# A Conformer block on one core: scores with keys on partitions, folded key weights and DMA transposes in place of the row-maximum softmax

## The chip, the cores and the metric

The kernel runs on one core of one Trainium2 chip. The metric is the device time of one execution in microseconds (us), the median of several runs. A core has five engines with a queue of instructions each: TensorE (PE in the profile, with its weight loads as PEld), VectorE (DVE), ScalarE (ACT), GpSimd (POOL) and SyncE (SP). Each queue is worked off in order. The engines meet through semaphores only.

## What is computed

```
x: 2 x 4000 x 512 bf16;  F = 2048;  LN(v) = (v - mean) / sqrt(var + 1e-5), no gain
x1 = x + 0.5 * silu(LN(x) @ w_ff1_a) @ w_ff1_b
h  = LN(x1);  q, k, v = h @ w_q, h @ w_k, h @ w_v
x2 = x1 + softmax(q k^T / sqrt(512)) v @ w_o            # one head, 4000 keys per batch
a, b = split(LN(x2) @ w_pw1);  g = a * sigmoid(b)
dc = depthwise conv of g over time, 3 taps (dw)
dc = (dc - mean) / sqrt(var + 1e-5) per channel, over all 8000 tokens
x3 = x2 + silu(dc) @ w_pw2
x4 = x3 + 0.5 * silu(LN(x3) @ w_ff2_a) @ w_ff2_b
out = LN(x4)
```

## The kernel before

The 8000 tokens are 64 tiles of 125 and 16 chunks of 500; a batch is 8 chunks. The residual stream (XT) stays in SBUF in bf16 with tokens on partitions. A small class (`Sync`) counts semaphores: each operation waits for what it reads and overwrites, in the order in which the program is written out. The block is four phases with barriers between them, and each phase allocates its own SBUF and PSUM.

**Layer norm** (L348 to L408). For each of a chunk's four tiles DVE takes statistics (`bn_stats` L353, `bn_aggr` L356); DVE adds epsilon (L359), and POOL makes the reciprocal root and the shift in three small operations (L362, L365, L368). ACT normalises each tile (L379). The features must then be on partitions: PE transposes each tile in four 125x128 pieces (L394, 16 to a chunk) into PSUM, and DVE copies them out (L407).

**Feed-forward, twice** (L460). For each chunk, 16 groups f: four matmuls (L533) make 128 hidden features by 500 tokens, ACT takes the sigmoid (L537), DVE multiplies (L540), and three groups later four matmuls (L555) add the group's share to four token tiles in PSUM. The residual enters through four more matmuls with twice the identity as weights (L551), and ACT copies the halved sum back to XT (L419). The layer norm of a chunk is prepared while the chunks before it are worked on.

**Attention** (L618). K^T, q^T and v' = h (Wv Wo) are projected for all chunks of a batch (L671, L696); q^T goes to DRAM and back (L687, L729). Then there are 128 tasks to a batch: a query tile of 125 against 1000 keys. PE makes scores with queries on partitions (L742), DVE takes their row maximum (L757) and updates the running one, ACT takes exp with the maximum as bias and sums (L787), PE transposes the eight blocks of probabilities (L818), DVE copies them (L827), PE multiplies by v' (L839), and DVE rescales and adds to the running output (L855). Scores are issued two tasks ahead.

**Convolution** (L1013). For each chunk: four pairs of gated projections (L1085, sigmoid L1089, product L1094), the layer norm of the next chunk mixed in between the pairs (one ACT normalisation behind each sigmoid), and the depthwise taps of two chunks before as diagonal matmuls (L1136), which ACT copies (L1140) and DVE takes statistics of (L1143). After all chunks the channel statistics are finished and a second loop does the normalisation, silu (L1205, L1209, L1213) and the last projection (L1229).

The order in one attention step and in one convolution step is written out by hand:

```
MX(n+1) EX(n+1) TR(n) CP(n) SC(n+2) PV(n) RL(n) OU(n-1)          # attention, task n
pw1_pair(tc, jj, lprev); stats at jj 0; transposes at jj 1 and 3   # convolution, chunk tc
```

Of the kernel before, what the change touches and what calls it, by code (L numbers as in the profile page):

```python
# [5 lines left out]
F32 = mybir.dt.float32  # L6
BF16 = mybir.dt.bfloat16
ALU = mybir.AluOpType
AF = mybir.ActivationFunctionType
AX = mybir.AxisListType  # L10

TILE = 125
CHUNK = 500
TPC = CHUNK // TILE
KEYBANK = 500
KBPC = 2
FF_LAG = 3
# [11 lines left out]
class Buf:  # L29
    __slots__ = ("name", "w", "r", "excl")  # L30
# [6 lines left out]

    def __repr__(self):
        return "Buf(%s)" % self.name


class Sync:
# [3 lines left out]
    def __init__(self, nc, n_dma_sems=32):  # L46
# [23 lines left out]
        self.stats = {"waits": 0, "instrs": 0, "multi": 0}  # L70

    def _required(self, reads, writes):
# [14 lines left out]
        for b in writes:  # L87
            add(b.w)
            for ev in b.r.values():
                add(ev)  # L90
        return req
# [9 lines left out]
    def _emit_waits(self, e, req):  # L101
        clk = self.clock[e]
        n = 0
        for key in sorted(req, key=str):
# [8 lines left out]
            n += 1  # L113
        self.stats["waits"] += n
        if n > 1:
            self.stats["multi"] += 1
# [8 lines left out]
    def op(self, e, fn, reads=(), writes=(), inc=True):  # L125
# [3 lines left out]
        self.stats["instrs"] += 1  # L129
# [21 lines left out]
    def dma(self, e, dkey, fn, reads=(), writes=()):  # L151
# [8 lines left out]
        self.stats["instrs"] += 1  # L160
# [13 lines left out]
    def barrier(self, engines=None):  # L174
        if engines is None:
            engines = self.ENGS
        targets = dict((k, v) for k, v in self.count.items() if v > 0)
        for e in engines:
            for key, val in targets.items():
                if key == e:  # L180
                    continue
                self.wait_event(e, Ev(key, val, {}))


def conformer_kernel(nc, x, w_ff1_a, w_ff1_b, w_q, w_k, w_v, w_o, w_pw1, dw, w_pw2,
                     w_ff2_a, w_ff2_b, out, phases=None):
    if phases is None:
        phases = dict(ff1=True, att=True, conv=True, ff2=True)
    B, T, D = x.shape
    F = w_ff1_a.shape[1]  # L190
    KW = dw.shape[0]
    N = B * T
    assert D == 512 and T % CHUNK == 0 and N % TILE == 0 and KW % 2 == 1 and KW < CHUNK
    DC = D // 128
    FC = F // 128
    NT = N // TILE
    NCK = N // CHUNK
    TCB = T // CHUNK
    TB = T // TILE
    SCALE = float(D) ** -0.5  # L200
    EPS = 1e-5
    PAD = KW // 2

    x_flat = x.rearrange("b t d -> (b t) d")
    out_flat = out.rearrange("b t d -> (b t) d")

    S = Sync(nc)
    uid = [0]

    def sbuf(stack, shape, dtype):  # L210
        uid[0] += 1
        return stack.enter_context(nc.sbuf_tensor("sb%d" % uid[0], shape, dtype))

    psum_banks = {}

    def psum(stack, shape, dtype):
        uid[0] += 1
        h = stack.enter_context(nc.psum_tensor("ps%d" % uid[0], shape, dtype))
        mloc = nc.lookup_mloc(h)
        psum_banks[h.name] = (mloc.bank, nc.num_psum_banks(shape, dtype))  # L220
        return h

    PSUM_PREFIXES = ("hps", "yps", "prj", "vpp", "sps", "ptp", "ops", "pwp", "dcps", "y2", "plnT", "dwps")

    def nbuf(prefix):
        uid[0] += 1
        return Buf("%s%d" % (prefix, uid[0]), excl=(prefix in PSUM_PREFIXES))

    with ExitStack() as gstack:
        XT = sbuf(gstack, [TILE, NT, D], BF16)  # L230
        bx = [Buf("x%d" % g) for g in range(NT)]
        ident = sbuf(gstack, [128, 128], BF16)
        bid = Buf("ident")
        ident2 = sbuf(gstack, [128, 128], BF16)
        bid2 = Buf("ident2")
        neghalf = sbuf(gstack, [128, 4], F32)
        bneghalf = Buf("neghalf")
        epsc = sbuf(gstack, [128, 4], F32)
# [9 lines left out]
        def _(_eng):  # L248
# [17 lines left out]
            def load_x(n_chunks):  # L266
                for _ in range(n_chunks):
                    tc = xload_state["next"]
                    if tc >= NCK:
                        return  # L270
# [1075 lines left out]
```

## Time and profile before

| | |
|---|---|
| device time, median of 3 runs | 2513.72 us (2510.93 to 2516.74) |
| span of the profiled execution | 2512.2 us |
| mean granted TensorE clock | 0.985 |
| PE busy | 95% of the span, 13220 matmuls |
| DVE busy | 71%, 4261 instructions |
| ACT busy | 47%, 2536 instructions |
| POOL busy | 5%, 255 instructions |
| DMA moved | 47.05 MB, all issued by SP |

The profile is of one execution, which lasted 2512.2 us from its first to its last instruction; the device time of the runs is about 1.5 us more. "busy" is the time in which an engine ran at least one instruction, and matmuls overlap each other. The chain of waits follows the work that ended last back in time, and says of each stretch which engine and line it was spent on. The timeline gives start and duration in us, engine, line, operation, operands and, in brackets, how long the engine had been idle before and for whom it waited. A window row gives for each engine the busy time and, in brackets, the instructions.

### The profile page before, as it was taken

The page shows a single profiled execution, that of the slowest core. Times are in us where ns is not written, and L with a number is a line of the kernel's source. Part 1 is how long each engine was busy: PE and PEld are TensorE (multiplying, and loading weights), DVE is VectorE, ACT ScalarE, POOL GpSimd, SP SyncE. Part 2 cuts the span into 40 slices and gives each one's busy share as a digit, 9 for nine tenths or more (in the row PEclk, how much of TensorE's full clock was granted, in tenths as well). Part 3 has the DMA queues.
Part 4 walks back from the last instruction along what each step waited for, and adds up shares of the span by engine and source line. Part 5 has one row for each costly group of instructions (what it writes and reads, how often), then busy time and mean ns, then how long its engine had stood idle before and what let it go on. Part 6 is the DMA issues. An engine that isn't in the chain of part 4 may idle for free.

```text
span 2512.2 us, 34795 instructions
## 1 busy us (share of the span) xinstructions
PE 2383.2 (95%) x13220; PEld 1429.3 (57%) x13220; DVE 1779.5 (71%) x4261; ACT 1185.9 (47%) x2536; POOL 115.2 (5%) x255
## 2 busy tenths in 40 slices
PE   5999999989999999989999999996998979999997
PEld 3555555544666666655566666664443545555554
DVE  4555555464888888887588888887887966666664
ACT  3544444444333333336433333333665845555554
POOL 0000000000000000001000000000110001000100
PEclk9999999999999999999999999998999989999999
DMA  4100000011000000001100000000000020000000
GB/s 156 43 1 1 1 1 1 4 63 51 9 9 9 9 9 9 1 1 42 42 9 9 9 9 9 9 1 26 1 1 1 1 68 17 17 17 19 23 17 25
DMA packets 44874, 47.05 MB, mean 19 GB/s; under 512 B 1057, under 2 KB 44196, under 8 KB 44708
## 3 DMA queue, kind: packets, MB, share of 16 engines
q1 hardware_dynamic: 44708, 44.83, 5.6%
q8 instruction: 105, 1.72, 0.3%
q14 instruction: 61, 0.50, 0.1%
HBM read 28.45 MB, written 16.38 MB: 18 GB/s over the span
## 4 chain that ended last, share of the span: by engine, by line
PE 90%; ACT 4%; DVE 3%; DMA 1%; SPq 1%; issue 1%; POOL 0%; ACTq 0%; POOLq 0%; DVEq 0%
PE ps L839 18%; PE ps L555 17%; PE ps L742 17%; PE ps L533 17%; PE ps L818 5%; PE ps L671 4%; PE ps L1085 3%; PE ps L394 2%; PE ps L1229 2%; ACT sb L379 1%; PE ps L1136 1%; PE ps L696 1%; PE ps L551 1%; DVE sb L353 1%; ACT sb L1089 1%; PE ps L1224 1%
## 5 line engine op out<-in xcount | busy, mean ns | idle before, releaser
L540 DVE TENSOR_TENSOR sb<-ps,sb 128x500 bf16<-128x500 f32 x512 | 339.8, 676 | 375.4 <-ACT sb L537 375.3
L555 PE MATMUL ps<-sb 128*125 128x512 bf16 x2048 | 525.9, 379 | 0.0
L533 PE MATMUL ps<-sb 128*128 128x500 bf16 x2048 | 510.5, 377 | 7.7 <-DVE sb L540 6.7
L839 PE MATMUL ps<-sb 125*125 125x512 bf16 x2048 | 485.2, 379 | 7.3 <-DVE sb L800 7.3
L742 PE MATMUL ps<-sb 128*125 128x500 bf16 x2048 | 478.1, 376 | 6.4 <-DMA sb<-qt_scratch 6.4
L537 ACT ACTIVATE sb<-ps 128x500 bf16<-128x500 f32 x512 | 300.9, 589 | 378.3 <-PE ps L533 366.8
L787 ACT ACTIVATE sb<-ps,sb 125x500 bf16<-125x500 f32 x512 | 339.0, 666 | 160.9 <-DVE sb L771 160.9
L555 PEld LDWEIGHTS ps<-sb 128*125 128x125 bf16 x2048 | 280.3, 137 | 173.2 <-issue 0.4
L839 PEld LDWEIGHTS ps<-sb 125*125 125x125 bf16 x2048 | 279.4, 137 | 168.3 <-DVE sb L800 8.7
L742 PEld LDWEIGHTS ps<-sb 128*125 128x125 bf16 x2048 | 260.6, 137 | 125.3 <-issue 10.8
L757 DVE TENSOR_REDUCE sb<-ps 125x1 f32<-125x1000 f32 x256 | 306.6, 1198 | 28.7 <-PE ps L742 21.5
L533 PEld LDWEIGHTS ps<-sb 128*128 128x128 bf16 x2048 | 196.7, 98 | 220.9 <-issue 12.3
L827 DVE COPY sb<-ps 125x1000 bf16<-125x1000 bf16 x256 | 174.8, 683 | 110.9 <-PE ps L818 110.9
L783 ACT ACTIVATE sb<-sb 125x1 f32<-125x1 f32 x192 | 38.9, 203 | 448.0 <-DVE sb L767 448.0
L379 ACT ACTIVATE sb<-sb 125x512 bf16<-125x512 bf16 x256 | 203.1, 804 | 52.3 <-POOL sb L368 52.3
L353 DVE BATCH_NORM_STATS2 sb<-sb 125x6 f32<-125x512 bf16 x320 | 213.2, 666 | 15.2 <-DMA sb<-in_x_dram 13.1
L407 DVE COPY sb<-ps 128x250 bf16<-128x250 bf16 x512 | 147.7, 289 | 80.2 <-PE ps L394 67.0
L362 POOL TENSOR_TENSOR sb<-sb 125x4 f32<-125x4 f32 x80 | 80.5, 1007 | 2339.4 <-DVE sb L359 2293.4
L818 PEld LDWEIGHTS ps<-sb 125*125 125x125 bf16 x2048 | 159.4, 138 | 44.6 <-ACT sb L787 4.5
L818 PE MATMUL ps<-sb 125*125 125x125 bf16 x2048 | 160.6, 222 | 3.4 <-ACT sb L787 3.4
L394 PE MATMUL ps<-sb 125*128 125x125 bf16 x1024 | 86.5, 224 | 63.5 <-ACT sb L379 58.0
L855 DVE SCALAR_TENSOR_TENSOR sb<-sb,ps 125x512 f32<-125x512 f32 x192 | 142.2, 740 | 2.3 <-PE ps L839 2.3
(78 smaller groups left out, 1826.6 us busy)
## 6 DMA issues: line engine op xcount, KB each, us to landing
qt_scratch<-sb SPq DMA_DIRECT2D x16, 500.0 KB, 3.7
sb<-qt_scratch SPq DMA_DIRECT2D x16, 500.0 KB, 3.7
sb<-in_x_dram SPq DMA_DIRECT2D x15, 500.0 KB
out_dram<-sb SPq DMA_DIRECT2D x15, 500.0 KB
sb<-in_w_ff_a_dram SPq DMA_DIRECT2D x8, 512.0 KB, 8.5
sb<-in_w_ff_b_dram SPq DMA_DIRECT2D x8, 512.0 KB, 8.6
sb<-in_w_pw_dram SPq DMA_DIRECT2D x1, 1024.0 KB, 5.3
sb<-in_w_q_dram SPq DMA_DIRECT2D x1, 512.0 KB, 4.1
```

The costliest lines, as they stand in the source:

```text
L353: ops.append(lambda ti=ti: S.op("DVE", lambda e, ti=ti: e.bn_stats(c.st[slot][:, ti, :], XT[:, g0 + ti, :]), reads=[bx[g0 + ti]], writes=[ ...
L379: ops.append(lambda ti=ti, g=g: S.op("ACT", lambda e: e.activation(c.lntm[slot][:, ti, :], XT[:, g, :], AF.Identity, bias=c.sh[slot][:, ti ...
L533: S.op("PE", lambda e, cc=cc, last=last: e.matmul(hps[r][:, 0:CHUNK], Wa[:, cc, f * 128:(f + 1) * 128], c.lnTsb[ls][:, cc, 0:CHUNK], start ...
L537: S.op("ACT", lambda e: e.activation(sig[ss][:, 0:CHUNK], hps[r][:, 0:CHUNK], AF.Sigmoid), reads=[b_hps[r]], writes=[b_sig[ss]])
L540: S.op("DVE", lambda e: e.tensor_tensor(out=h1T[slot][:, f, 0:CHUNK], in0=hps[r][:, 0:CHUNK], in1=sig[ss][:, 0:CHUNK], op=ALU.mult), reads ...
L555: S.op("PE", lambda e, ti=ti: e.matmul(yps[ti][:, :], h1T[slot][:, fp, ti * TILE:(ti + 1) * TILE], Wb[:, fp, :], start=False, stop=lastf), ...
L742: S.op("PE", lambda e, cc=cc, kk=kk, kbk=kbk, last=last: e.matmul(sps[sset][:, kk, 0:KEYBANK], qTb[qslot][:, cc, qt * TILE:(qt + 1) * TILE ...
L757: S.op("DVE", lambda e: e.tensor_reduce(pm[p][:, :], sps[sset][:, 0:nkb, 0:KEYBANK], AX.XY, ALU.max), reads=[b_sps[sset][kk] for kk in ran ...
L787: S.op("ACT", lambda e, kk=kk: e.activation(Psb[pp][:, kk * KEYBANK:(kk + 1) * KEYBANK], sps[sset][:, kk, 0:KEYBANK], AF.Exp, bias=negm[p] ...
L818: S.op("PE", lambda e, kc=kc: e.transpose(ptp[pp][:, kc, 0:TILE], Psb[pp][:, kc * TILE:(kc + 1) * TILE], ident[:TILE, :TILE]), reads=[b_P[ ...
L827: S.op("DVE", lambda e: e.tensor_copy(PT[pp][:, 0:nb, 0:TILE], ptp[pp][:, 0:nb, 0:TILE]), reads=[b_ptp[pp]], writes=[b_PT[pp]])
L839: S.op("PE", lambda e, kc=kc, last=last: e.matmul(ops[pp][:, :], PT[pp][:, kc, 0:TILE], Vp[:, k0 + kc, :], start=(kc == 0), stop=last), re ...
```

## The change

The kernel is written anew as one class; what it computes stays the same, and a second copy of the whole program is kept behind a flag. Memory is laid out once, and there is no barrier between stages: buffers that share memory know of each other (`alias`), and operations wait on that basis. Work is put off by counted steps: `lags` holds matmul groups that run some steps later, and `after(n, fn)` holds small work for the n-th `tick`.

- **Layer norm.** DVE normalises (a subtract and multiply by per-token scalars), except in the convolution, where ACT does it as before. Each 125-token tile is then turned by one `dma_start_transpose` from SP, 128x512 from SBUF to SBUF, in place of the four PE transposes and the DVE copies. There are four such DMAs to a chunk and layer norm, eight in the first feed-forward, which makes both its own input and the attention keys.
- **Feed-forward.** ACT takes silu in one operation, straight into bf16. The residual is added by one DVE operation on each output tile (`residual`), without identity matmuls.
- **Attention.** `fold_weights` makes M = Wq Wk^T and Wvo = Wv Wo. Keys are the normalised features (hT), values the normalised tokens (h); only q M is projected. Scores have 128 key rows (125 and three of zero) on partitions and 500 queries in the free dimension, exp is taken without a maximum, DVE adds up the probabilities (`acc`), and four matmuls add the values to four PSUM banks. At the end of a query chunk the sums go through eight one-column matmuls, and the output is projected by Wvo and scaled as it is added to the residual.
- **The flag.** The sum of squares of M bounds the scores; if it is over a limit, the second copy of the program, which takes row maxima, runs after the first.
- **Convolution.** `pop` here issues one depthwise group (three matmuls, ACT's copy, DVE's statistics). The four PSUM banks of `sbank` are taken in turn, one for each half of a pair. The whole layer norm of the next chunk is put behind the first pair of a chunk (`gap=0`). The channel statistics are collected as before; the silu and the last projection of the first four chunks come after them, those of the others inside the second feed-forward.
- Weights of the first feed-forward are loaded in 16 DMAs by ACT's queue, and x by SP's.

The parts that the prediction speaks of:

```diff
+    def transpose(self, dst, src, reads, writes):
+        k = self.S.dsems[12 + self.nxt("tr", 16)]
+        return self.S.dma("SP", k, lambda e: e.dma_start_transpose(dst, src), reads=reads, writes=writes)
...
+    def ln_job(self, c, at, kind, eng="DVE", gap=1):
+        sl = self.nxt("ln", self.LN_SLOTS)
+        def tile(ti):
...
+            self.ln_norm(c, sl, ti, tok[0:TILE, :], b_tok, eng)
+            self.transpose(feat, tok, [b_tok], [b_feat])
+        t = at
+        for ti in range(TPC):
+            self.after(t, lambda ti=ti: self.ln_stats(c, sl, ti))
+            if ti % 2:
+                t += gap
+        self.after(t, lambda: self.ln_aggr(c, sl, eng == "ACT"))
+        t += 2 * gap
+        for ti in range(TPC):
+            self.after(t, lambda ti=ti: tile(ti))
+            if ti % 2:
+                t += gap
...
+    def ff_chunk(self, c, old, hook, done):
+        pops = {0: old // 2, 1: old - old // 2, 2: 0, 3: 0, 7: 2, 11: 2}
+        for f in range(FC):
+            ps, b_ps = self.sbank()
...
+            for cc in range(DC):
+                self.mm(out, self.Wa[:, cc, f * 128:(f + 1) * 128], self.lnT[c % 2][:, :, cc, 0:TILE],
+                        cc == 0, cc == DC - 1, [self.b_Wa[f * self.NWA // FC]] + self.b_lnT[c % 2], b_ps)
+            self.act(self.P[s], ps[:, 0:CHUNK], AF.Silu, [b_ps], [self.b_P[s]])
...
+            self.lags.append(second)
+            self.pop(pops.get(f, 1))
+            hook(f)
+            self.tick()
...
+            for kt in range(TB):
...
+                for cc in range(DC):
+                    self.mm(ps[:, 0:CHUNK], self.hT[kc][:, kj, cc, :], self.qT[s][:, cc, :],
...
+                self.act(self.P[p], ps[:, 0:CHUNK], AF.Exp, [b_ps], [self.b_P[p]], scale=SCALE)
...
+                    S.op("DVE", lambda e, p=p: e.tensor_tensor(
+                        out=self.acc[s], in0=self.acc[s], in1=self.P[p], op=ALU.add),
...
+                def values(kt=kt, p=p, qc=qc):
+                    for dc in range(DC):
+                        self.mm(self.Yb[dc][:, 0:CHUNK], self.h[kt][:, dc * 128:(dc + 1) * 128], self.P[p],
...
+                    if kt == TB - 1:
+                        self.finish_queries(b, qc, done)
+
+                self.lags.append(values)
...
+    def finish_queries(self, b, qc, done):
+        S, s = self.S, qc % 2
+        for dc in range(DC):
+            if dc % 2:
+                S.op("DVE", lambda e, dc=dc: e.tensor_copy(self.OT[:, dc, :], self.Yb[dc][:, 0:CHUNK]),
...
+                self.act(self.OT[:, dc, :], self.Yb[dc][:, 0:CHUNK], AF.Copy, [self.b_Y[dc]], [self.b_OT[dc]])
+        S.op("DVE", lambda e: e.tensor_copy(self.ahi, self.acc[s]), reads=[self.b_acc[s]], writes=[self.b_ahi])
+        S.op("DVE", lambda e: e.tensor_tensor(out=self.alo, in0=self.acc[s], in1=self.ahi, op=ALU.subtract),
...
+        self.after(2, sums)
+        for ti in range(TPC):
+            self.after(4 + ti, lambda ti=ti: project(ti))
...
+    def conv(self, old, hook):
+        S = self.S
+        for t in range(NCK):
+            gs, gp = t % self.NG, (t - 1) % self.NG
+            for jj in range(DC):
+                halves = []
+                for cb in (DC + jj, jj):
+                    ps, b_ps = self.sbank()
...
+                self.act(self.sig[ss], pb[:, 0:CHUNK], AF.Sigmoid, [b_pb], [self.b_sig[ss]])
+                S.op("DVE", lambda e, pa=pa, ss=ss, jj=jj, gs=gs: e.tensor_tensor(
+                    out=self.G[gs][:, jj, 1:1 + CHUNK], in0=pa[:, 0:CHUNK], in1=self.sig[ss], op=ALU.mult),
...
+                self.halo(t, jj)
...
+                elif t > 1 or jj > 1:
+                    self.pop(1)
+                hook(t, jj)
+                self.tick()
...
+        def conv_hook(t, jj):
...
+            if jj == 0 and t + 1 < NCK:
+                self.ln_job(t + 1, 0, "in", "ACT", gap=0)
+
+        self.conv(old, conv_hook)
+        self.drain()
+        for k in range(4):
+            self.load_wb(i["w_ff2_b"], 4 * k, 4 * k + 4)
+        AHEAD = 4
+        for t in range(AHEAD):
+            for cc in range(DC):
+                self.swish(t, cc)
+            for ti in range(TPC):
+                self.pw2(t, ti)
+            if t == 0:
+                self.ln_job(0, 0, "in", gap=0)
+                self.tick()
```

More of the change, by code (lines that the diff above doesn't have):

```diff
@@ L7 @@
 BF16 = mybir.dt.bfloat16
+I32 = mybir.dt.int32
 ALU = mybir.AluOpType
@@ L10 @@
 AX = mybir.AxisListType
+B, T, D, F, KW = 2, 4000, 512, 2048, 3
 TILE = 125
@@ L14 @@
 TPC = CHUNK // TILE
-KEYBANK = 500
-KBPC = 2
-FF_LAG = 3
+N = B * T
+NT = N // TILE
+NCK = N // CHUNK
+TCB = T // CHUNK
+TB = T // TILE
+DC = D // 128
+FC = F // 128
+EPS = 1e-5
+SCALE = float(D) ** -0.5
+SCORE_LIMIT = 60.0
 class Ev:
@@ L90, in _required @@
                 add(ev)
+            for a in b.alias:
+                add(a.w)
+                for ev in a.r.values():
+                    add(ev)
         return req
```

1686 lines of the change are left out of this document (620 added, 1066 removed).

## The prediction

> **What bounds the kernel now.** I read the page first, then windows by stage, then the chain of waits inside a feed-forward chunk and an attention task. The page says that PE is the bound:
>
> ```profile
> PE 2383.2 (95%) x13220; PEld 1429.3 (57%) x13220; DVE 1779.5 (71%) x4261; ACT 1185.9 (47%) x2536; POOL 115.2 (5%) x255
> PE 90%; ACT 4%; DVE 3%; DMA 1%; SPq 1%; issue 1%; POOL 0%; ACTq 0%; POOLq 0%; DVEq 0%
> ```
>
> The windows (first feed-forward; first attention loop; convolution; last projection; second feed-forward) show where that holds: 463 of 465 us and 487 of 494 in the first two, but 177 of 214 in the convolution.
>
> ```profile
> 33.90:499.00 465.10, 463.35 (x2332) 260.09 (x2332) 248.96 (x510) 222.46 (x380) 21.79 (x48) 1.00 0.04 14
> 613.00:1107.00 494.00, 486.96 (x2985) 330.62 (x2986) 416.76 (x1041) 190.49 (x597) 2.81 (x6) 0.99 0.03 8
> 1724.00:1938.00 214.00, 176.78 (x964) 80.10 (x964) 174.34 (x450) 121.36 (x193) 23.86 (x51) 0.95 0.03 8
> 1938.00:2035.00 97.00, 80.58 (x350) 46.24 (x351) 78.98 (x195) 67.64 (x105) 4.01 (x8) 0.89 0.14 44
> ```
>
> The chain (start, length) gives the price of a matmul:
>
> ```profile
> 58.04 3.45 PE ps L555 x16
> 62.78 2.53 PE ps L533 x12
> 87.12 3.45 PE ps L555 x16
> ...
> 710.73 0.46 PE ps L818 x8
> 711.19 1.69 PE ps L742 x8
> 712.88 1.73 PE ps L839 x8
> 714.61 0.46 PE ps L818 x8
> ```
>
> A 500-column matmul takes 2.53/12 = 0.2108 us, a 512-column one 3.45/16 = 0.2156, a transpose 0.46/8 = 0.0575. A feed-forward chunk has 64, 68 and 16 of them: 13.49 + 14.66 + 0.92 = 29.07, and its period is 87.12 - 58.04 = 29.08. An attention task is 0.46 + 1.69 + 1.73 = 3.88, its period 714.61 - 710.73 = 3.88. There PE waits for nothing, so the new time is first PE's new work, then each place where PE would wait.
>
> **PE's work after the change.** These groups go, or shrink:
>
> ```profile
> L818 PE MATMUL ps<-sb 125*125 125x125 bf16 x2048 | 160.6, 222 | 3.4 <-ACT sb L787 3.4
> L671 PE MATMUL ps<-sb 128*128 128x500 bf16 x512 | 116.1, 374 | 2.5 <-DVE sb L407 2.4
> L394 PE MATMUL ps<-sb 125*128 125x125 bf16 x1024 | 86.5, 224 | 63.5 <-ACT sb L379 58.0 <-DVE sb L407 2.9 <-DVE sb L863 1.9
> L551 PE MATMUL ps<-sb 125*125 125x512 bf16 x128 | 49.0, 383 | 0.0
> ```
>
> At the pitches above: probability transposes 2048 x 0.0575 = 118 us, layer-norm transposes 59, one of the two projections 256 x 0.2108 = 54, identity matmuls 28. The new count is taken from the code.
> Feed-forward: 32 chunks of 64 + 64: 32 x (13.49 + 13.80) = 873.3.
> Attention: 16 query chunks of 256 score and value matmuls (53.97), 16 for the next q (3.37), 16 of 512 columns for the output (3.45), 8 sums at the transpose's price (0.46): 16 x 61.25 = 980.0.
> Folding: 32 x 0.2156 = 6.9. Convolution: 704 x 0.2108 = 148.4. Last projection: 256 x 0.2156 = 55.2.
> Sum 2063.8 us. DVE's maxima, copies and rescaling (L757, L827, L855) go with the old softmax; in their place are one addition for each key tile and, elsewhere, residuals. DVE and ACT stay under PE in the big stages: a key tile gives PE 8 x 0.2108 = 1.69 us, ACT one exp of about 0.6, DVE one addition below the 0.74 of L855:
>
> ```profile
> L855 DVE SCALAR_TENSOR_TENSOR sb<-sb,ps 125x512 f32<-125x512 f32 x192 | 142.2, 740 | 2.3 <-PE ps L839 2.3
> L680 DVE CAST sb<-ps 128x500 bf16<-128x500 f32 x64 | 41.7, 674 | 18.3 <-PE ps L671 16.7 <-issue 0.2
> L1209 DVE TENSOR_SCALAR sb<-sb 128x500 bf16<-128x500 bf16 x64 | 25.9, 405 | 2.0 <-POOL sb L1192 2.0
> ```
>
> **Where PE waits: convolution.** This is the largest term. The new order puts the next chunk's whole layer norm behind the first pair. ACT is in order, so its four normalisations stand ahead of the second pair's sigmoid and wait for statistics and for POOL. The timeline of the old convolution's start, then of its last chunk, gives each piece:
>
> ```profile
> 1730.57 0.66 DVE L353 BATCH_NORM_STATS2 sb<-sb 125x6 f32<-125x512 bf16 x1
> ...
> 1731.48 0.17 DVE L359 TENSOR_SCALAR sb<-sb 125x4 f32<-125x4 f32 x1
> 1731.82 1.01 POOL L362 TENSOR_TENSOR sb<-sb 125x4 f32<-125x4 f32 x1 [545.03 <-DVE sb L359]
> ...
> 1733.49 2.92 ACT L379 ACTIVATE sb<-sb 125x512 bf16<-125x512 bf16 x4 [15.98 <-POOL sb L368]
> ```
>
> ```profile
> 1916.06 6.91 PE L1085 MATMUL ps<-sb 128*128 128x500 bf16 x32
> ...
> 1917.11 0.59 ACT L1089 ACTIVATE sb<-ps 128x500 bf16<-128x500 f32 x1 [0.26 <-PE ps L1085]
> 1918.02 0.68 DVE L1094 TENSOR_TENSOR sb<-ps,sb 128x500 bf16<-128x500 f32 x1 [0.45 <-PE ps L1085]
> ```
>
> Set a chunk's first matmul at 0. The product of pair 0 ends at 2.6 (1918.02 + 0.68 - 1916.06). A depthwise group follows (three matmuls 0.63, ACT's copy 0.6 and DVE's statistics 0.67, by the rows of L1089 and L353), to 3.9 on DVE. Four layer-norm statistics at 0.66 end at 6.55. From the last statistics to ACT's start is 1733.49 - 1731.23 = 2.26, plus 0.3 for three more aggregations: 9.1. Four normalisations, 2.92: 12.1. Only now comes pair 1's sigmoid (12.7). PE has meanwhile done pairs 1 and 2 with their depthwise groups and stops at 7.0, as pair 3 needs the bank that this sigmoid reads. PE thus idles 5.8 us, then has pair 3 and a depthwise group (2.3): 15.1. And it starts cold:
>
> ```profile
> 33.90 1.82 PE L533 MATMUL ps<-sb 128*128 128x500 bf16 x4 [5.32 <-DVE sb L540]
> ```
>
> After 5.3 us idle four matmuls took 1.82 us, 0.455 each instead of 0.211; I charge 1.9 for the eight of pair 3, so the period is 17.0. [...] Fifteen periods of 17.0 and a last one of about 10 make 265, against 148.4 of work: **+117**. The old period bounds the gain side:
>
> ```profile
> 1798.66 2.54 PE ps L1085 x12
> ...
> 1810.41 2.54 PE ps L1085 x12
> ```
>
> 11.75 us, where each normalisation lies behind a sigmoid and not ahead of three.
>
> **DMA transposes.** No row shows one. The nearest are x tiles of the same 125 KB, and for the dear side a transfer of 500 KB in scattered pieces:
>
> ```profile
> 0.74 1.47 SPq L278 DMA_DIRECT2D sb<-in_x_dram  x4
> ...
> 4.12 0.69 DVE L353 BATCH_NORM_STATS2 sb<-sb 125x6 f32<-125x512 bf16 x1 [4.12 <-DMA sb<-in_x_dram]
> ```
>
> ```profile
> 607.93 5.38 DMA sb<-qt_scratch
> ```
>
> So an issue costs 1.47/4 = 0.37 and landing 4.12 - 0.74 = 3.4; on the dear side a tile could hold the queue 5.4. I take the x tile's, as size and shape are its own. In the convolution the last tile then lands at 12.1 + 0.37 + 3.4 = 15.9, inside the period of 17. In the first feed-forward eight transposes (3 us of issue) lie in a chunk of 27.3; a chunk's input is turned in its steps 5 to 7 of 16 and needed at its end, so some 14 us hide it. SP holds nothing else urgent there: one x load per chunk. If T is the time that a transpose holds the queue, cover is gone when 8T > 27.3.
>
> **Other waits.** Start: statistics of four tiles end near 8.5 with weights sharing the DMA engines, root by 10.5, four DVE normalisations (0.4 each) and the last landing, 17 for PE's first matmul; cold start 2, by the cold row. The folded weights: three large transposes have 10 us from issue to use; I charge 3 (0 to 10). End of a query chunk: four PSUM copies in turn on ACT and DVE (0.6 and 0.67), behind the exp and addition of that step, free the last bank 0.6 us late, and the sums wait for `ahi` and `alo` about 0.9: 1.5 x 16 = 24; first queries of a batch 1 x 2. At the joint from convolution to last projection PE idled 5.9 us before (below); four silus of about 0.6 now stand ahead of the first full group: 8. Later DVE's in-order layer norm of chunk 0 holds the residuals that free the banks, 6 more: 14 (9 to 20). The feed-forward itself should wait for nothing: its four residuals (4 x 0.74) start as each bank finishes, and three groups of 0.84 lie between. Tail: residual, statistics, root, normalisation and store as before, from the last matmuls to the end. The joint, then the tail:
>
> ```profile
> 1938.50 0.66 PE L1224 MATMUL ps<-sb 125*125 125x512 bf16 x1 [5.87 <-POOL sb L1192]
> ...
> 2495.65 3.62 PE L555 MATMUL ps<-sb 128*125 128x512 bf16 x16
> ...
> 2505.42 2.90 SPq L509 DMA_DIRECT2D out_dram<-sb  x4
> ```
>
> The last matmul ends near 2499.2, the span at 2512.2: 13.
>
> **Sum.** 2063.8 + 17 + 2 + 3 + 24 + 2 + 117 + 14 + 13 = 2255.8 of span. The profiled execution spans 2512.2 and the median of the runs is 2513.7, so I add 1.5: **2257 us**.
>
> **Rivals.**
> A. The convolution loses no more than it does now: period 11.75, 15 x 5.25 = 79 less, 2178. For it: this trace keeps that period with the same matmuls and 16 transposes more. Against: the order on ACT.
> B. T between 2 and 4 us, tiles one after another. Normalised tiles start to appear at 9.9 in a convolution chunk, so its period becomes 9.9 + 4T + 3.4: at T = 3, 25.3, and 15 x 8.3 = 125 more: 2382. The feed-forward still hides 24 of 27.3.
> C. Slower than before: SP's transposes become the bound. Each chunk of the first feed-forward costs 8T, each convolution period 13.3 + 4T. The extra is 16 (8T - 27.3) + 15 (4T - 3.7) = 188T - 492, and uses up the 257 us of gain at T = 4.0. At the scratch row's 5.4: 523 more, 2780. For it: 256 such DMAs where no row prices one. Against: the x tiles' 0.37. [...]
> D. The flag is not set and the second copy runs, over twice 2257. Weight entries are near 0.0022, M's sum of squares near 0.003, the limit 7.
>
> **How the numbers follow.** Forecast 0.61 (its own range 2190 to 2340, from the convolution's 13 to 20 us periods, the fold and the joint to the second feed-forward), A 0.13, B 0.15, C 0.09, D 0.01, no change 0.01. The range 2170 to 2400 leaves out C, D, the upper part of B and the lower edge of A. The runs of before spread 0.12% about their median, so 0.2% is what can be told from no change. Faster 0.88, same 0.01, slower 0.11 (C, D and what I have not thought of).
>
> **What would show it.** Right: feed-forward chunks of 27.3 us, query chunks of 61 to 63, PE's matmuls near 9,830; in the convolution ACT's normalisation waits for POOL for 5 to 6 us in each chunk, PE for ACT's sigmoid about as long, and the granted clock dips. Wrong: feed-forward chunks over 28 with PE waiting for a DMA transpose (B, C); convolution periods near 12 (A); PE waiting for `acc` or the residuals inside a stage.

## The result and the profile after

The changed kernel takes **2277.59 us** (median of 4 runs, 2276.55 to 2278.29) beside 2515.23 for the kernel before on the same chip: ratio **0.9056, 95% interval 0.9043 to 0.9069**. The forecast was 2257, with 2170 to 2400 as the range. The profiled execution spans 2274.3 us and lasted 2278.08.

The page after: the engines, the chain by engine, and the DMA transposes of the layer norms (count, median us from issue to landing).

```profile
PE 2131.4 (94%) x9828; PEld 1063.6 (47%) x9830; DVE 989.3 (43%) x2013; ACT 804.1 (35%) x1362; POOL 122.0 (5%) x283
PE 87%; DVE 6%; ACT 3%; issue 2%; POOL 1%; DMA 1%; SPq 0%; POOLq 0%; DVEq 0%; ACTq 0%
work<-work SPq DMA_TRANSPOSE x192, 2.5
```

PE is still the bound. It is busy 251.8 us less than before and the span is 237.9 us shorter: the gain is PE's missing work, and the time in which PE does nothing has grown by 14 us. The windows of the changed kernel (first batch's feed-forward and attention, convolution, joint, second feed-forward, tail) say where that idle time lies. A row gives its length, the busy time of PE, PEld, DVE, ACT and POOL, the granted clock, the DMA share and GB/s:

```profile
35.70:266.00 230.30, 230.20 (x1062) 124.22 (x1065) 72.91 (x201) 82.91 (x146) 13.11 (x13) 1.00 0.28 59
266.00:768.00 502.00, 496.50 (x2370) 232.56 (x2369) 234.32 (x378) 172.02 (x294) 2.01 (x2) 1.00 0.02 4
1480.00:1750.20 270.20, 200.40 (x745) 82.21 (x743) 131.01 (x283) 113.33 (x190) 39.14 (x173) 0.82 0.15 32
1750.20:1776.87 26.67, 16.72 (x65) 9.46 (x66) 18.02 (x37) 13.31 (x18) 2.02 (x2) 0.87 0.39 99
1776.87:2257.10 480.23, 480.21 (x2241) 266.43 (x2239) 196.35 (x502) 180.39 (x304) 30.25 (x30) 1.00 0.14 33
2257.10:2274.30 17.20, 0.00 (x0) 0.00 (x0) 6.07 (x17) 0.00 (x0) 1.01 (x1) 0.58 0.11 33
```

The feed-forward windows are full. The convolution's 745 matmuls are 157 us at 0.2108, so 113 of its 270 us are waiting or half clock. The first window begins at 35.70: nothing runs on PE before. Two rows of the chain, one chunk apart in the first feed-forward, and two of DVE's timeline, one query chunk apart in the attention, give the periods 27.41 and 62.68:

```profile
129.59 2.55 PE s L435 x12
...
157.00 2.55 PE s L435 x12
...
331.66 0.68 DVE L666 TENSOR_TENSOR work<-work 128x500 bf16<-128x500 f32 x1
...
394.34 0.68 DVE L666 TENSOR_TENSOR work<-work 128x500 bf16<-128x500 f32 x1
```

One period of the convolution in the timeline, then the two waits over the whole run (us in all, times, longest):

```profile
1591.72 2.93 ACT L439 ACTIVATE work<-xt,work 125x512 bf16<-125x512 bf16 x4 [5.26 <-POOL work L486]
1592.56 5.12 SPq L447 DMA_TRANSPOSE work<-work  x4
1594.56 0.56 ACT L439 ACTIVATE wff<-s 128x500 bf16<-128x500 f32 x1
1595.17 3.51 PE L435 MATMUL s<-work 128*128 128x500 bf16 x8 [4.67 <-ACT wff L439]
1599.73 1.04 PE L435 MATMUL s<-work 128*128 128x500 bf16 x2
```

```profile
ACT work L439 <- POOL work L486: 79.2, 15, 5.5
PE s L435 <- ACT wff L439: 64.1, 14, 4.7
```

ACT waits 5.3 us for the root, normalises four tiles (2.93), and only then takes the sigmoid (1594.56) for which PE has waited 4.7 us; PE restarts at half clock (0.50 granted from 1595.17 to 1598.68), 3.51 us for eight matmuls in place of 1.7. The last transpose goes out at about 1596.4 and by the page's 2.5 lands at 1598.9, 0.8 us before the next chunk's first matmul (1599.73).

The start, in the timeline:

```profile
13.86 14.99 POOL L869 MEMSET keys<- 128x512 bf16 x32
13.94 16.01 DVE L492 TENSOR_SCALAR work<-xt,work 125x512 bf16<-125x512 bf16 x4 [1.15 <-POOL work L479]
29.02 5.22 SPq L447 DMA_TRANSPOSE work<-work  x4
35.70 4.74 PE L435 MATMUL s<-work,wff 128*128 128x500 bf16 x11 [35.70 <-DMA work<-work]
```

Four normalisations that cost 0.4 us each elsewhere take 16 us, and end at 29.95, 1.1 us after POOL's 32 memsets of the key tiles (28.85).

### The profile page after: what moved, and what is told of

Read it like the earlier page. It is cut to its first block, busy times and chain, and to the rows that moved or that the text cites. A ratio compares the mean times of both kernels' runs of the same rounds, so it can differ in the third digit from the quotient of the medians.

```text
span 2274.3 us, 24679 instructions
## 1 busy us (share of the span) xinstructions
PE 2131.4 (94%) x9828; PEld 1063.6 (47%) x9830; DVE 989.3 (43%) x2013; ACT 804.1 (35%) x1362; POOL 122.0 (5%) x283
## 4 chain that ended last, share of the span: by engine, by line
PE 87%; DVE 6%; ACT 3%; issue 2%; POOL 1%; DMA 1%; SPq 0%; POOLq 0%; DVEq 0%; ACTq 0%
PE s L435 49%; PE y L435 38%; ACT work L439 2%; DVE work L469 2%; POOL work L479 1%; DVE work L661 1%; DVE work L492 1%; DVE wff L749 1%; DVE work L666 0%; DMA xt<-in_x_dram 0%; DVE work L635 0%; ACT keys L439 0%; ACT wff L439 0%; DVE work L475 0%; DVE work L665 0%
## 5 line engine op out<-in xcount | busy, mean ns | idle before, releaser
L439 ACT ACTIVATE work<-s 128x500 bf16<-128x500 f32 (+1 forms) x1068 | 626.5, 587 | 1270.2 <-PE s L435 1265.1
L435 PE MATMUL y<-wff,work 128*125 128x512 bf16 (+1 forms) x2240 | 574.2, 384 | 0.0
L435 PE MATMUL s<-work,wff 128*128 128x500 bf16 x2048 | 511.2, 378 | 35.7 <-DMA work<-work 35.7
L635 DVE TENSOR_TENSOR work<-work 128x500 f32<-128x500 f32 x496 | 336.9, 679 | 474.1 <-ACT work L439 473.2
L435 PE MATMUL y<-work,keys 128*128 128x500 bf16 x2048 | 519.0, 374 | 2.0
L435 PE MATMUL s<-work,keys 128*128 128x500 bf16 x2048 | 517.4, 375 | 0.3
L435 PEld LDWEIGHTS y<-wff,work 128*125 128x125 bf16 (+1 forms) x2240 | 301.2, 134 | 204.2 <-issue 11.2
L435 PE MATMUL s<-work 128*128 128x500 bf16 (+3 forms) x1158 | 296.6, 393 | 87.6 <-ACT wff L439 64.1
L435 PEld LDWEIGHTS s<-work,wff 128*128 128x128 bf16 x2048 | 200.9, 98 | 258.0 <-issue 39.2
L435 PEld LDWEIGHTS y<-work,keys 128*128 128x128 bf16 x2048 | 198.1, 97 | 244.5 <-DVE work L661 15.3
L469 DVE BATCH_NORM_STATS2 work<-xt 125x6 f32<-125x512 bf16 x320 | 200.3, 680 | 7.5 <-DMA xt<-in_x_dram 7.5
```

Of the source, the lines that this page charges most:

```text
L435: self.S.op("PE", lambda e: e.matmul(out, lhsT, rhs, start=start, stop=stop), reads=reads, writes=[bank], inc=stop if inc is None else inc)
L439: return self.S.op("ACT", lambda e: e.activation(out, in_, func, **kw), reads=reads, writes=writes)
L469: self.S.op("DVE", lambda e: e.bn_stats(self.st[sl][:, ti, :], self.XT[g]), reads=[self.bx[g]], writes=[self.b_st[sl][ti]])
L635: S.op("DVE", lambda e, p=p: e.tensor_tensor(out=self.acc[s], in0=self.acc[s], in1=self.P[p], op=ALU.add), reads=[self.b_P[p], self.b_acc[ ...
```

## The experiments

All are edits of the changed kernel. Two heads occur: the first matmul comes at 35.2 to 35.7 us (DVE held, as above) or at 28.1 to 28.9. In the profiled executions it is the late one but for `c3_zero_spread`, `c7_no_second`, `c13_norms_together` and `c8_best`; where 7 us matter, spans of the same head are compared.

The theory that went in: in the convolution the normalisations at the head of ACT's queue set the period of 17.0 us. Rivals: the DMA transposes set it, or the late request for the statistics does.

**Normalise on DVE** (`c1_norm_dve`)

```diff
-                self.ln_job(t + 1, 0, "in", "ACT", gap=0)
+                self.ln_job(t + 1, 0, "in", "DVE", gap=0)
```

> In the convolution stage the four normalisations of the next chunk go to DVE in place of ACT; everything else stays. Theory (ACT's queue: the normalisations wait about 5.3 us for the statistics and the root, and pair 1's sigmoid stands behind them): ACT is free, DVE waits only about 1.4 us for the root and does four times 0.41 us; the period of a chunk falls from 17.05 to 12 to 13 us, the stage by 60 to 75 us, the kernel to about 2210 us (2200 to 2225); PE's wait for ACT's sigmoid falls from 4.7 to under 1.5 us and its clock no longer dips. Rival (the transposes on SP's queue, 1.27 us each to issue and 2.5 to land, bound the period): it stays at 17, within 5 us of 2277.

Measured 2263.12 us (2260.76 to 2271.53). Both expectations missed: the theory's 2200 to 2225 by far, and the rival's "within 5 us of 2277" by some 9. The profiled execution is the slowest of the four; its span is 6.7 us under that of the changed kernel, with the same late head, and all of that lies in the first four chunks. The timeline of one chunk, and the wait:

```profile
1650.86 1.38 DVE L492 TENSOR_SCALAR work<-xt,work 125x512 bf16<-125x512 bf16 x4 [1.13 <-POOL work L479]
1651.30 5.12 SPq L447 DMA_TRANSPOSE work<-work  x4
1657.96 3.49 PE L435 MATMUL s<-work 128*128 128x500 bf16 x8 [3.41 <-issue]
```

```profile
PE s L435 <- DMA work<-work: 65.5, 10, 35.3
```

ACT no longer blocks, but now PE's first matmul of the next chunk (1657.96) waits for the transposes: the last of the four lands at about 1657.6 by the page's 2.5, though this row names no releaser. Ten waits name it, and without the first of the program they are 65.5 - 35.3 = 30 us. In this stretch the period did not move. The row of SyncE's timeline that groups eleven chunks' transposes shows it for the changed kernel, then for this one:

```profile
1558.56 175.60 SPq L447 DMA_TRANSPOSE work<-work  x44
```

```profile
1548.70 176.20 SPq L447 DMA_TRANSPOSE work<-work  x44
```

Without the last chunk's 5.1 us that is 10 periods of 17.05 and of 17.1. Ahead of that stretch, up to 1550 us, the periods of this execution are 15.3 to 16.4 at a granted clock of 0.92; in it the clock is 0.80. The other three executions took 2260.76 to 2264.53 us at a mean clock of 0.983 to 0.985, against 0.976 in this one. An early head would explain 7 us of that, but not the clock, which in `c2_stats_ahead` is 0.991 to 0.992 with either head. No profile shows the periods of these three; by estimate from these figures they stayed at some 16.2. That is still far from the theory's 12 to 13.

**PE transposes in the convolution, with DVE or ACT normalising** (`c10_pe_dve`, `c11_pe_act`)

```diff
-            self.transpose(feat, tok, [b_tok], [b_feat])
+            if kind == "conv":
+                self.after(2, lambda: self.pe_transpose(feat, tok, [b_tok], b_feat))
+            else:
+                self.transpose(feat, tok, [b_tok], [b_feat])
```

> In the convolution stage alone the next chunk's tiles are normalised on DVE and transposed by PE (16 transposes of 0.06 us a chunk, issued two pairs later, and four copies by DVE of about 0.4 us) in place of ACT and SP's DMA transposes. One of four corners: ACT or DVE normalises, DMA or PE transposes; both corners with DMA transposes have a period of 17.0 us. Theory (two loops of nearly one length: ACT's queue behind the normalisations, and statistics, root, normalisation, 6.7 us of four DMA transposes, first matmul of the next chunk; each has to go before the other shows): period 11.5 to 13 us, the kernel 65 to 85 us under the changed kernel, 2195 to 2215. Rival (only statistics and root asked for at the chunk's start, whoever normalises or transposes, set 17): within 15 us of 2265.

> The same with the normalisations left on ACT: in the convolution stage PE transposes the tiles, ACT normalises. Theory of two loops: ACT's queue still holds pair 1's sigmoid for 5.3 us of waiting and 2.9 us of normalising, so the period stays at 16 to 17.5 and the kernel within 15 us of 2277. Rival (the DMA transposes alone set the 17): period 11 to 13, 2200 to 2215.

Measured 2269.37 (2267.39 to 2270.14) and 2301.83 us (2301.74 to 2301.87). For `c10_pe_dve` the rival was right. The first and the last of eleven roots on POOL, then a stretch between them:

```profile
1552.52 1.01 POOL L489 TENSOR_TENSOR work<-work 125x4 f32<-125x4 f32 x1 [3.75 <-DVE work L487]
...
1716.44 1.01 POOL L489 TENSOR_TENSOR work<-work 125x4 f32<-125x4 f32 x1 [3.75 <-DVE work L487]
```

```profile
1652.31 1.38 DVE L502 TENSOR_SCALAR work<-xt,work 125x512 bf16<-125x512 bf16 x4 [1.13 <-POOL work L489]
1653.61 0.67 DVE L723 TENSOR_TENSOR wff<-s,wff 128x500 bf16<-128x500 f32 x1
...
1655.95 1.40 DVE L456 COPY work<-s 128x512 bf16<-128x512 bf16 x4
1656.41 3.51 PE L435 MATMUL s<-work 128*128 128x500 bf16 x8 [0.30 <-DVE work L456]
```

The period varies from 15.4 to 17.0 and is 16.4 in the mean. With ACT and the DMA both out of the way, the products and the copies now stand behind the normalisations on DVE, and PE's pair 3 behind those. `c11_pe_act` keeps ACT's wait and puts the 16 PE transposes into the same chain: period 18.4, 10 us over its expectation's upper end; that the DMA transposes alone set the 17 is out.

**Statistics a chunk ahead** (`c2_stats_ahead`, `c13_norms_together`)

```diff
-            if jj == 0 and t + 1 < NCK:
-                self.ln_job(t + 1, 0, "in", "ACT", gap=0)
+            if t == 0 and jj == 0:
+                self.ln_job(1, 0, "in", "ACT", gap=0)
+            if t + 2 < NCK:
+                if jj == 0:
+                    ahead[t + 2] = self.nxt("ln", self.LN_SLOTS)
+                self.ln_stats(t + 2, ahead[t + 2], jj)
+                if jj == DC - 1:
+                    self.ln_aggr(t + 2, ahead[t + 2], True)
+            if t > 0 and t + 1 < NCK and jj < 2:
+                for ti in (2 * jj, 2 * jj + 1):
+                    self.ln_norm(t + 1, ahead[t + 1], ti, self.ltm[ti][0:TILE, :], self.b_ltm[ti], "ACT")
...
```

In `c13_norms_together` the last condition is `jj == 0`, and the loop takes all four tiles.

> In the convolution stage the statistics and the root of chunk t+2 are made during chunk t, one tile a pair, and the normalisations stay on ACT, two ahead of each of the first two pairs; nothing is left out. Theory (what costs is ACT standing at the head of its queue for statistics and root that are asked for too late): the wait for POOL goes, the period falls to 10 to 10.5 us, the stage loses 100 to 105 us, the kernel comes to about 2173 us (2165 to 2185). Rival 1 (four normalisations of 0.73 us on ACT are themselves the cost): the period falls only to 14 to 15, about 2235. Rival 2 (SP's transposes bound): it stays at 17, 2277.

> As the run with the statistics a chunk ahead, but the four normalisations stand together behind the first pair's sigmoid as they do in the changed kernel: only the statistics and the root are asked for earlier. Theory (the cost is the loop from a chunk's first pair through statistics, root and normalisation to the next; asked for a chunk ahead it is cut, and 2.9 us of normalising on ACT at once is carried by four score banks): period 10 to 11 us, the kernel 2180 to 2200. Rival (it was the spreading of the normalisations, two to a pair, that gave the gain): period 13 to 15, 2225 to 2260.

Measured 2187.92 (2184.66 to 2191.62; ratio to before 0.8698, interval 0.8682 to 0.8713) and 2192.98 us (2188.50 to 2196.80; 0.8728, 0.8711 to 0.8745). The same row of SyncE's timeline, `c2_stats_ahead` first:

```profile
1534.62 110.83 SPq L447 DMA_TRANSPOSE work<-work  x44
```

```profile
1528.99 115.71 SPq L447 DMA_TRANSPOSE work<-work  x44
```

The periods are about 10.6 and 11.1 against 17.05; `c2_stats_ahead` is 3 us over its expected range, `c13_norms_together` inside its theory's. In `c13_norms_together` ACT still normalises four tiles at a time in front of the sigmoids, and the DMA still transposes: asking earlier for statistics and root is alone worth 85 us by the medians, and about 80 in the profiled executions without the 7 us of the early head. Asked for a chunk ahead, the four statistics also lie one to a pair and no longer in a row on DVE; no run has the one without the other. The granted clock recovers with it; 100 us of the convolution, the changed kernel and then `c2_stats_ahead`:

```profile
1560.00:1660.00 100.00, 74.18 (x264) 29.66 (x264) 47.89 (x102) 40.75 (x70) 15.04 (x66) 0.80 0.16 32
```

```profile
1560.00:1660.00 100.00, 90.25 (x420) 40.21 (x418) 72.10 (x149) 65.36 (x111) 21.87 (x104) 1.00 0.22 44
```

**Keep PE warm** (`c5_keep_warm`)

```diff
-                    for cc in range(DC):
+                    for rep in range(4 if jj == 2 else 1):
+                        for cc in range(DC):
```

> In the convolution stage the matmuls of the third pair are done four times over (same result, written again), 24 extra matmuls of 0.21 us a chunk, to fill the idle stretch ahead of the fourth pair and keep PE's clock up. Theory A (the half clock behind the 4.7 us idle stretch costs about 3 us a chunk on the chain): the granted clock stays at 1.00 there, the 0.44 us matmuls go, period 14.5 to 16, the kernel 15 to 40 us faster than 2277. Theory B (the loop through statistics, root, normalisation and DMA transposes sets 17 and the cold matmuls lie beside it): within 6 us of 2277. Theory C (the extra work is itself in the way of the pair behind it): 5 us a chunk more, up to 2360.

Measured 2270.01 us (2268.84 to 2270.71). The clock of the stage is 1.00 and the roots on POOL come every 15.8 us:

```profile
1553.04 1.01 POOL L479 TENSOR_TENSOR work<-work 125x4 f32<-125x4 f32 x1 [3.76 <-DVE work L477]
...
1711.19 1.01 POOL L479 TENSOR_TENSOR work<-work 125x4 f32<-125x4 f32 x1 [3.76 <-DVE work L477]
```

So the half clock costs 1.2 us a chunk on the loop, and not the 3 of theory A; then PE waits up to 1.2 us for the transposes. The period is inside A's range, but the 7.6 us gained are under A's 15 and over B's 6. Up to the last root of the loop the execution is 15.5 us ahead, and half of that is lost again behind it: from that root to the next one, in the second feed-forward's first layer norm, it is 44.8 us in place of 40.2, about the 5 us of 24 extra matmuls, and 3 more follow up to the root after that.

**Each transpose twice** (`c4_transpose_twice`)

```diff
             self.transpose(feat, tok, [b_tok], [b_feat])
+            self.transpose(feat, tok, [b_tok], [b_feat])
```

> Each DMA transpose of a layer-norm tile is issued twice, the same data to the same place; the weights' transposes stay single. It prices the transposes. Theory (hidden in the feed-forward and in front of the queries; in the convolution the last tile's lands a good 6 us before its matmuls want it): the first and second feed-forward keep their 27.4 and 30 us a chunk; in the convolution four more issues of 1.27 us each put the last landing about 5 us later, which the period of 17 still covers or nearly covers: 0 to +20 us, head +5 us, so 2282 to 2302. Rival (the transposes bound the period): each chunk of the convolution grows by 5.1 us, +82 us, about 2360.

Measured 2513.07 us (2508.72 to 2521.09), ratio to before 0.9996 (0.9984 to 1.0008): no gain is left of the whole change. Both expectations missed, since the second copy writes where the first does and waits for it to land on SP's queue. The chain (start, length) in the first feed-forward:

```profile
147.64 7.68 DMA work<-work
...
156.57 2.49 DMA work<-work
...
159.08 1.19 SPq L447
...
160.31 2.49 DMA work<-work
...
184.19 7.10 DMA work<-work
```

A tile holds the queue 160.31 - 156.57 = 3.74 us there, and from the first tile of one chunk to that of the next, with the waits ahead and one x load, it is 184.19 - 147.64 = 36.55 us, 4.6 for each of eight. This brings about rival C of the prediction: it said that T = 4.0 uses up the gain, and at 3.7 to 4.6 the gain is gone. In parts it fits less well. About 79 us are lost ahead of the convolution, where C charges 75 at T = 4.0; in the convolution, at a period of 27.3, it is 141 and not C's 185; and 21 us lie behind it, where C has nothing. In the changed kernel, as the 5.12 for four above shows, T is 1.28.

**PE transposes everywhere** (`c6_pe_transpose`). Every `self.transpose` of a layer-norm tile becomes four PE transposes and one DVE copy, up to two steps later.

> Every layer-norm tile, in all stages, is transposed by PE and copied out by DVE in place of the DMA; the weights' transposes stay DMA. It undoes that part of the change. PE gets 256 tiles of four transposes at about 0.06 us each, 61 us, and DVE 256 copies of about 0.4 us, 102 us beside PE. Theory (the DMA transposes are hidden outside the convolution and the head): feed-forward and keys cost 50 to 60 us more, the head gets 4 to 6 us shorter, the convolution stays: 2320 to 2340. Rival (the DMA transposes or their waits cost time in the feed-forward too): under 2300.

Measured 2343.94 us (2342.79 to 2344.30): 66 us more, 4 over the expected range. The chain's rows of two chunks in the first feed-forward:

```profile
133.52 2.55 PE s L435 x12
162.72 2.55 PE s L435 x12
```

29.20 a chunk in place of 27.41: 32 transposes at 0.0575 are 1.84. There the DMA transposes are hidden entirely, and PE's are not. About 27 of the 66 us lie ahead of the convolution and 20 behind its last root. The other 20 are the convolution's, which the expectation took as unchanged: its period is 18.4, as in `c11_pe_act`.

**Memsets spread** (`c3_zero_spread`)

```diff
-            self.S.op("POOL", lambda e, k=k: e.memset(self.h[k], 0.0), writes=[self.b_h[k]])
+            self.after(1 + k // 2, lambda k=k: self.S.op("POOL", lambda e: e.memset(self.h[k], 0.0),
+                                                      writes=[self.b_h[k]]))
```

> The 32 memsets of the key tiles go out two to a tick of the program, after the first normalisations, in place of all at the head of POOL's queue. Theory (DVE's four normalisations at the head took 16.0 us in place of 1.6 because POOL's memsets held them): the first matmul comes at 20 to 22 us in place of 35.7 and the kernel falls by 13 to 16 us, to about 2262. Rival (the head waits for the x tiles and the weights on their way in, and the normalisations would have been late anyway): the first matmul stays past 30 us and the time within 4 us of 2277. If later memsets now hold DVE in the first feed-forward chunks, up to 10 us of the gain come back there.

Measured 2270.65 us (2268.02 to 2273.22): 7 less, between the two. An early head also occurs with the memsets as they were (`c7_no_second`, `c13_norms_together`), so the profile alone does not credit the edit; but the slowest of these four executions is below the fastest of the changed kernel's four. Eight memsets still lay beside the normalisations (3.34 us for the four), the first matmul came at 28.64, and the four transposes took 9.29 us to issue in place of 5.2, beside the weights' transfers and the next x load.

**No second program** (`c7_no_second`). The flag's load, the branch and the second program are left out.

> The flag is still worked out but not read, and the second program behind it is left out of the kernel; for inputs like these the result is the same. It prices that part of the tail. Theory (SP reads the flag and branches behind the last output transfer, and the rest of the tail is the last normalisation and its transfers): 2 to 4 us less, 2274. Rival 1 (the second program's code is fetched or set up beside the first): 10 us or more less. Rival 2: nothing, within 1 us.

Measured 2273.28 us (2266.74 to 2274.80). The ratios, 0.9047 (0.9035 to 0.9060) and 0.9056 (0.9043 to 0.9069), overlap, so the times do not settle it. The time outside the span does in part: it is 1.2 to 1.3 us in all five executions (2266.74 - 2265.5 in the profiled one) and 3.7 to 3.9 in all four of the changed kernel. Still, the second program is not enough for the 2.5: `c6_pe_transpose` keeps it and has 1.7 to 1.8 outside. The tail behind the last matmul is 0.5 us shorter, in one profiled execution each. Its head, unexpectedly, was the early one with nothing changed there:

```profile
13.52 15.57 POOL L869 MEMSET keys<- 128x512 bf16 x32
13.61 3.34 DVE L492 TENSOR_SCALAR work<-xt,work 125x512 bf16<-125x512 bf16 x4 [1.15 <-POOL work L479]
28.85 6.36 PE L435 MATMUL s<-work,wff 128*128 128x500 bf16 x20 [28.85 <-DMA work<-work]
```

The same 32 memsets held DVE for 3.3 us here and for 16.0 there.

**Row maxima** (`c9_row_max`). `self.program(True)` is run in place of `self.program(False)`, without the flag's branch.

> The program with row maxima (the one behind the flag) is run in place of the first, alone. It undoes the part of the change that drops the row maximum, in the new layout. Per query chunk it adds 64 matmuls for the maxima and 32 that subtract them, 96 at about 0.21 us, 20.3 us on PE, 325 us over 16 chunks, and on DVE 16 reductions of about 0.7 us beside them with a serial run of small steps at the end of each tile. Theory: 350 to 480 us more, 2630 to 2760, slower than the kernel before, so that dropping the maximum is worth more than the whole gain. Rival (the maxima lie beside other work): under 2600.

Measured 3131.43 us (3125.88 to 3134.22), ratio to before 1.2458 (1.2438 to 1.2478): the sign was right, the size not. The end of one tile's maxima and the end of the next but one, on DVE:

```profile
509.95 0.28 DVE L608 CAST work<-s 3x125 bf16<-3x125 f32 x1 [0.31 <-PE s L435]
...
531.81 0.28 DVE L608 CAST work<-s 3x125 bf16<-3x125 f32 x1 [0.31 <-PE s L435]
```

10.93 us a tile. The expectation counted 64 matmuls to a query chunk where there are 128 (4 query tiles, 8 key chunks, 4 each: 27.0 us), and 4 us to a tile stand bare: small serial steps on DVE (0.15 to 0.28 us each), and matmuls at lower pace behind PE's pause (granted clock 0.84 from 507.90 to 529.80). Four tiles and 32 subtracting matmuls are 43.7 + 6.7 = 50.4 a query chunk; 53.4 were measured. With maxima taken in this way the new layout would be slower than the old kernel.

**Three edits together** (`c8_best`): `c2_stats_ahead` with two of the four normalisations in the pair before, the memsets behind the second chunk's root (`5 + k // 2`), and `self.after(3, sums)` in place of 2.

> Three changes on the changed kernel, nothing left out: statistics of the convolution's layer norm a chunk ahead and half of the normalisations a pair earlier still; the 32 memsets behind the second chunk's root on POOL; the row sums one step later. Theory: the convolution comes to about 9.9 us a chunk and gives 95 to 105 us, the first matmul comes at 25 to 28 us in place of 35.7 and gives 8 to 10, the row sums 5 to 8: 2155 to 2170. Rival (the head is bound by the DMA transposes beside the weights' transfers, whatever DVE does): the head gives 4 to 7 only and the row sums nothing, 2172 to 2182.

Measured **2168.16 us** (2164.77 to 2172.36), ratio to before 0.8629 (0.8613 to 0.8644), 109 us under the changed kernel. Period 10.2; from the first matmul to the convolution some 6.5 us less than in `c2_stats_ahead`, about the 7.8 us in 16 waits for `alo` (L666) there, of which 0.7 are left. The head:

```profile
13.44 1.38 DVE L492 TENSOR_SCALAR work<-xt,work 125x512 bf16<-125x512 bf16 x4 [1.15 <-POOL work L479]
13.88 10.32 SPq L447 DMA_TRANSPOSE work<-work  x4
28.13 6.94 PE L435 MATMUL s<-work,wff 128*128 128x500 bf16 x20 [28.13 <-DMA work<-work]
```

With DVE free the normalisations take 1.38 us, and the transposes become the bound: 10.32 us to issue beside the weights' transfers and the next x load, against 5.22 at 29.02 in the changed kernel. No run moves those transfers, so that they are the cause is argued. 28.1 is the earliest first matmul seen.

## Why the prediction was right, and where it was not

| step | forecast | measured |
|---|---|---|
| feed-forward chunk | 27.3 | 27.41 |
| query chunk | 61.25 + 1.5 | 62.68 |
| start | 17 | 35.7 |
| folded weights | 3 | 0 |
| period in the convolution | 17.0 | 17.05 |
| joint, idle | 14 | 26.67 - 65 x 0.2108 = 13 |
| second feed-forward, with 192 matmuls of the last projection | 16 x 27.29 + 192 x 0.2156 = 478 | 480.2 |
| tail | 13 | 17.2 |
| outside the span | 1.5 | 3.8 |

**PE's work at the pitches of before: right.** It is the whole gain, 9,828 matmuls against 13,220, and it set both feed-forwards and the attention to within 1%.

**The convolution: the number right, the reason half right.** The prediction's chain (statistics, root, four normalisations on ACT, then pair 1's sigmoid, PE idle and cold) is in the trace piece by piece. But it read ACT's order as the cause. Freeing ACT (`c1_norm_dve`) left 17.1 in most of the profiled execution and by estimate some 16 in the others, as the transposes of four tiles (1.28 us each on the queue, 2.5 to land) closed a second loop of nearly the same length; freeing both (`c10_pe_dve`) left 16.4, as DVE's and PE's order closed a third. What they share is the stretch from a chunk's first product through statistics and root to the normalisation. Taken out of the loop by asking a chunk ahead, it gives 6 us a chunk (`c13_norms_together`), with ACT's order and the DMA as they were. The 1.9 us charged for the cold clock were 1.8 on the eight matmuls (3.51 in place of 1.7) and 1.2 on the loop. That 17.0 met 17.05 so closely is therefore in part luck.

**The DMA transposes: hidden, as forecast, and mis-sized.** 0.37 us of issue was 1.28, 3.4 to land was 2.5. The prediction gave the last landing at 15.9 of a period of 17; by the trace the slack is 0.8 us. At T = 1.28 the eight of a chunk of the first feed-forward hold the queue for 10.2 of its 27.41 us; rival C's break-even lay at 4.0.

**The start: the term that was wrong, 18.7 us.** Without memsets (`c8_best`) the four normalisations end at 14.8 in place of 12.1, as the x tiles land later: 2.7. From there to the first matmul it is 13.3 us in place of 4.9, the transposes beside the weights' transfers and the next x load: 8.4. The last 7.6, from 28.1 to 35.7, are DVE held by POOL's memsets. The prediction did not name the memsets at all. The four normalisations took 16.01 us beside 14.99 us of memsets, against 1.38 in `c8_best`, where none lay beside them. That the queue of 32 held DVE is read from these times; no run shows the cause, and in `c7_no_second` the same queue held it for 3.34 us only.

**The tail: 4.2 short.** The prediction took the store as before, where four issues took 2.90 us (its row of L509). Here they take 8.43, and SyncE waits three times in between for the store ahead to land:

```profile
2263.46 8.43 SPq L808 DMA_DIRECT2D out_dram<-work  x4
```

```profile
SPq L808 <- DMA out_dram<-work: 7.1, 3, 2.7
```

The code says why: the last chunk goes out in four DMAs that all name one buffer as written (`b_out`), so the program orders them by landing. That is 5.5 us more, and covers the 4.2. No run undoes it.

**Time outside the span: 2.3 short.** It is 1.2 to 1.3 us without the second program, but also only 1.7 to 1.8 with it and PE transposes (`c6_pe_transpose`); what the 2.5 us come from stays open.

The errors of one sign (start, tail, outside: 25 us) stand against some 5 the other way in the fold, the joint and the convolution: 2277.6 against 2257.

**Rivals.** A's period of 11.75 needed the normalisations behind sigmoids; `c13_norms_together` (11.1 us) shows that they need not be, if the root is there. B's formula counts one T too many, as the landing runs from the issue of the last tile; with three, and the measured figures, 9.9 + 3 x 1.28 + 2.5 = 16.2 is the second loop. C's break-even of 4.0 is borne out in the total by `c4_transpose_twice`, its split over the stages only roughly.

## What to carry to other kernels

When a period is a loop over engines, moving one step to another engine may show only the next loop of nearly the same length (17.05 us here, then some 16.2 to 17.1, then 16.4); look for the stretch that all of them share and take it out of the loop by asking for it an iteration ahead (11.1). Ask of every term hidden by a small margin what hides it, and count the head's transfers at the price they have beside the weights (9.3 to 10.3 us to issue four transposes here, against 5.2). Housekeeping on an idle engine, such as memsets, can hold a busy one (16.0 us for four normalisations beside the memsets in most profiled executions here, 3.3 in others, 1.38 without). Where a program orders its transfers by the buffers that they write, give parts that do not overlap names of their own.

## What the runs showed of the hardware

- A DVE `tensor_scalar` on bf16 beside a run of POOL memsets: 0.35 us alone (1.38 for four), 16.0 for four in some executions and 3.3 in others of the same instructions, with the memset starting 0.08 to 0.09 us earlier both times (16.0 in the changed kernel, 3.3 in `c7_no_second` and `c13_norms_together`). In `c8_best` a single one took 14.97 us. What decides between the two was not found.
- A DMA transpose of a 128x512 bf16 tile holds SP's queue 1.28 us and lands after 2.5; at the start, beside the weights and an x load, four take 9.3 to 10.3 us to issue, and 5.2 where they start at 28.6 to 29.0.
- After 4.7 us idle PE's next eight matmuls take 0.44 us each in place of 0.21, at a granted clock of 0.50 (changed kernel, 1595.17 to 1598.68).
